# Attention scores with 64-row by 32-column TensorE tiles in place of zero-padded queries

## Chip, cores and metric

The kernel runs on one core of a Trainium2 chip. The metric is the device time of one execution in microseconds, as the median over runs. All times below are in microseconds (us) unless marked ns.

## What is computed

The program is three blocks in a row: a windowed attention, a mixture of experts and a dense block with a rational activation. The change touches the attention alone. Cut to it, the reference is

```python
B, H, Sl, D, Sg = 4, 8, 512, 64, 32
k_all, v_all = concat([k_g, k_l]), concat([v_g, v_l])
out_g = softmax(q_g @ k_all.T / 8) @ v_all             # 32 global tokens see everything
s_ll = q_l @ k_l.T / 8, kept where |i - j| <= 32        # local tokens see a window
s_lg = q_l @ k_g.T / 8                                  # and the 32 global tokens
out_l = softmax(concat([s_lg, s_ll])) @ concat([v_g, v_l])
attn = concat([out_g, out_l])                          # (4, 8, 544, 64)
x = attn as (2176, 512); x = experts(x); out = dense(x)
```

Everything is float32.

## The kernel before

**Tiling.** A batch has 512 local tokens, cut into 16 blocks of 32 (`W`). A block of queries needs 128 keys: three blocks of local keys and the 32 global ones. `KT[b]` holds the transposed keys: two heads of a pair stand on partitions 0 to 63 and 64 to 127, four pairs along the free axis, and the global keys are repeated between the local blocks so that 128 neighbouring columns are what a query block needs. `QB0` and `QB1` (`qb_t`, L305) hold the transposed queries, scaled by -1/8, of one half of a batch each. They are padded: for each pair and block there are two groups of 32 columns, the first with queries on partitions 0 to 63 and zeros below, the second the other way round. So one stationary operand of 128 rows by 64 columns gives the scores of both heads of a pair against their own keys.

**One unit** (`unit`, L565) is four query blocks of one batch, all eight heads; there are 4 per batch, 16 in all. It runs two halves `hg` of four heads. Each half takes one of four PSUM banks of the ring `sc`, adds the window mask by one bf16 matmul of 128x128 by 512 columns (L589), then runs 8 matmuls (L596) of 128x64 by 128 columns, each into 64 of the 128 partitions:

```python
nc.tensor.matmul(ps[64*j:64*j+64, n*128:(n+1)*128],
                 qb_t[u//2][:, 2*hg+j, u%2*4+n].rearrange("p a q -> p (a q)"),
                 KT[b][:, 2*hg+j, o:o+128], start=False, stop=True, ...)
```

The trace writes two records for each float32 matmul, so a half is 16 records of L596. `weights` (L604) then takes the row maximum on DVE (`mx`, L609), four exponentials on ACT (`A`, L285), frees the bank, transposes on PE (L627) and copies (`AT`). `values` multiplies with the value windows `VW` (L650: 32 float32 matmuls of 128x32 by 64 columns, four column groups), normalizes (L661, `xs`), stores to `xd`, and computes router logits (L679, L694, L703).

**Global queries.** `globals_of` (L714) does the same for the 32 global queries of a batch: per half two matmuls of 128x64 by 512 columns (L729) and two by 32 (L732), from `qgT`, which is zero-padded too. `prep_g` (L459) makes `kgT` and `qgT`: a copy that brings the heads into the order `ORD` (on DVE for k, on POOL for q, L464), four transposes (L471), copies out of PSUM on ACT.

**Order of work.** Nothing is left to a hardware scheduler. `Flow` is a planner that runs at build time: each piece of work is a Python generator that yields `(engine, us)` before it issues, and the planner keeps a clock for each engine and issues by rank and by earliest start. Its assumed costs therefore set the order on PE, ACT, DVE, POOL and SP, and each engine then works strictly in that order. A half of a unit's scores is planned as `("PE", 1.3)`. Transfers go through SP: keys, queries, values (`kr`, `qr`, `vr`), window copies from SBUF to SBUF (`VW<-vr`), stores (`xd`), and between them 24 pieces of the dense block's weights (`stg`, 512 KB each, three buffers), which ACT (L264) and DVE (L265 to L267) turn from 64-bit into 32-bit during the attention. The second planner run (router, experts, dense block) begins with a clock of its own and is issued after the attention's last PE and ACT instructions.

Of the kernel before, what the change touches and what calls it, by code (L numbers as in the profile page):

```python
# [66 lines left out]


class Flow:

# [18 lines left out]
    def _on(self, p, got=None):  # L89
        gen, rank, after, _ = p  # L90
        self.now = after
        while True:
# [5 lines left out]
            if isinstance(item, Ring):  # L98
                if item.waiters or not item.free():
                    item.waiters.append(p)  # L100
                    return
                got = self._take(item, after)
            elif isinstance(item, Slots):
# [85 lines left out]
def moe_kernel(ctx: ExitStack, tc: tile.TileContext, q_l, k_l, v_l, q_g, k_g, v_g, w_gate, w1, w2,  # L189
# [81 lines left out]
    with ExitStack() as actx:  # L271
# [186 lines left out]

        def prep_g(key, eng):  # L459
            yield g_in[key]  # L460
            yield eng, 0.6
            t, g = graw[key]
            src = raw.tile([128, H, D], F32, name=f"{key}g", tag="gr", bufs=1)
            (V if eng == "DVE" else nc.gpsimd).tensor_copy(src.rearrange("p (a c) d -> p a c d", a=2),  # L464
                                                           t.rearrange("p (c a) d -> p a c d", a=2))
            flow.fire(g)
            sc = yield sc_s
            p = bank("sc", 4)
            yield "PE", 0.436
            for pr in range(NP):  # L470
                nc.tensor.transpose(p[:, pr * 128:(pr + 1) * 128],  # L471
                                    src[:, 2 * pr:2 * pr + 2, :].rearrange("p h d -> p (h d)"), identf)
            p = p.rearrange("p (a s) -> p a s", a=NP)
            if key == "k":
                yield "ACT", 0.48
                act(kgT, p, AF.Copy)
            else:
                for h in range(2):
                    yield "ACT", 0.48
                    o = slice(64 * h, 64 * h + 64)  # L480
                    act(qgT[o, :, :, h], p[o].rearrange("p a (b q) -> p a b q", b=B), AF.Copy)
            flow.fire(g_t[key])
            flow.fire(sc)

        def pairs_T(src, s, put, done, rank):

            t = src.rearrange("p h (t d) -> p h t d", t=2)
            for par in range(2):
# [3 lines left out]
                for pr in range(NP):  # L492
                    for a in range(2):
                        nc.tensor.matmul(p[64 * a:64 * a + 64, pr * 128:(pr + 1) * 128], t[:, ORD[2 * pr + a], par],  # L494
                                         identf, start=True, stop=True)
# [11 lines left out]
        def both_T(src, s, put, done, rank):  # L507

            for a in range(2):
# [3 lines left out]
                for pr in range(NP):  # L513
                    nc.tensor.transpose(p[:, pr * 128:(pr + 1) * 128], src[:, ORD[2 * pr + a]], identf)
                if a:
# [37 lines left out]
        def prep_q(b, r, rank):  # L553
# [4 lines left out]
            t = qb_t[r]  # L558

            def put(a, par, rows, p):  # L560
                o = t[rows, :, :, a].rearrange("p a n (q t) -> p a n q t", t=2)
                copy(o[:, :, :, :, par], p.rearrange("p a (n q) -> p a n q", n=8), -scale)

# [3 lines left out]
        def unit(b, u, rank):  # L567
# [12 lines left out]
            flow.go(after(A_free, a), 0)  # L580
            flow.go(values(b, u, rank, at, sm, m, turned), rank)
            for hg in range(2):
                sc = yield sc_s
                ps = bank("sc", 4)
                yield "PE", 1.3
                m0 = 2 if u else 0
                ms = masks[:, m0:m0 + 4] if u in (0, NB // 4 - 1) else \
                    masks[:, None, m0:m0 + 2].to_broadcast([128, 2, 2, 128])
                nc.tensor.matmul(ps.rearrange("p (a n) -> p a n", n=128) if ms.ndim == 3 else  # L589
                                 ps.rearrange("p (a b n) -> p a b n", a=2, b=2), identh, ms,  # L590
                                 start=True, stop=False, skip_group_check=True)
                for n in range(4):
                    w0 = win(4 * u + n)
                    o = (w0 // 2 * 3 + w0 % 2) * W
                    for j in range(2):
                        nc.tensor.matmul(ps[64 * j:64 * j + 64, n * 128:(n + 1) * 128],  # L596
                                         qb_t[u // 2][:, 2 * hg + j, u % 2 * 4 + n].rearrange("p a q -> p (a q)"),
                                         KT[b][:, 2 * hg + j, o:o + 128], start=False, stop=True,
                                         skip_group_check=True)
                flow.fire(k_used[b, 0])  # L600
                flow.fire(q_used[b, u // 2])
                flow.go(weights(rank, hg, ps, sc, A[:, hg], mx[:, hg], sm, at, at_in, turned, A_free),
                        rank + 0.01 * hg)
# [105 lines left out]
        def globals_of(b, rank):  # L709
# [6 lines left out]
            for hg in range(2):  # L716
# [8 lines left out]
                yield "PE", 1.0  # L725
                lq = [qgT[:, 2 * hg + j, b].rearrange("p a q -> p (a q)") for j in range(2)]
                kt = sl(KT[b])[:, 2 * hg:2 * hg + 2]
                for j in range(2):
                    nc.tensor.matmul(ps[64 * j:64 * j + 64].rearrange("p (g s) -> p g s", s=2 * W), lq[j],  # L729
                                     kt[:, j, :, :2 * W], start=True, stop=True)  # L730
                for j in range(2):
                    nc.tensor.matmul(pg[64 * j:64 * j + 64, :SG], lq[j], kt[:, j, 0, 2 * W:], start=True, stop=True)  # L732
                flow.fire(k_used[b, 0])
# [117 lines left out]
        with tc.manual_schedule(engines={ET.PE, ET.Activation, ET.DVE, ET.SP, ET.Pool}):  # L851
            warm(W1)
            flow.clock["PE"] = 0.52 * W1
            flow.go(load_global(k_g, "k"), -9)
            flow.go(prep_g("k", "DVE"), -9)
            for b in range(B):
# [10 lines left out]
                if b == 0:  # L867
                    flow.go(load_global(q_g, "q"), 2 - LD[0])
                    flow.go(prep_g("q", "POOL"), 1)
                for u, n in ((0, i), (1, i + 1), (2, i + 3), (3, i + 4)):  # L870
# [902 lines left out]
```

## Time and profile before

| | |
|---|---|
| runs | 879.29 median of 3 (878.82 to 881.04) |
| the profiled execution | 881.8, of which 880.0 is its span |
| mean granted TensorE clock | 0.973 of full speed |
| busy share of the span | PE 94%, DVE 81%, ACT 57%, POOL 30% |
| attention | from the start to about 192 |

A group's row gives a line, an engine, the operation, the tile written and those read, sizes and count; behind the bar the busy time, the mean of one in ns, and idle time before the group with what ended it. Busy times of overlapping matmuls are merged. A timeline row gives start, length (first start to last end), engine, line, operation and count. A chain row gives start and length of a step on the chain of waits, which is followed back from the last instruction. A row of windows gives, for each stretch, busy time and count per engine, the granted clock (1.00 is 2.4 GHz, 0.50 is 1.2 GHz), the DMA engines' busy share and GB/s.

### The profile page before, as it was taken

How to read it: one execution, taken by the hardware profiler on the slowest of the kernel's cores; microseconds unless marked ns; L12 is line 12 of the kernel's file. 1: busy time of each engine (PE TensorE's matmuls, PEld its weight loads, DVE VectorE, ACT ScalarE, POOL GpSimd, SP SyncE). 2: the span in 40 equal slices, each digit the busy share in tenths (PEclk: the TensorE clock that was granted, in tenths of full speed). 3: DMA queues.
4: the chain of work that ended last, by engine and by line, in shares of the span. 5: the costliest groups of instructions: out<-in, count | busy, mean ns of one | idle time of the engine just before them, and what ended most of it. 6: DMA issues, size and time to landing. Idle time of an engine off the chain costs nothing.

```text
span 880.0 us, 20528 instructions
## 1 busy us (share of the span) xinstructions
PE 830.7 (94%) x7945; PEld 730.3 (83%) x7956; DVE 712.1 (81%) x1647; ACT 504.1 (57%) x1137; POOL 260.8 (30%) x227
## 2 busy tenths in 40 slices
PE   8887988879899999999999999999999999999997
PEld 5665766657689899999889999998999999998995
DVE  4557777758889989989998989999887767668985
ACT  4665676759544545545554554555455555556753
POOL 7510220000223334233442433334243343330001
PEclk9998997989999999999999999999999999999999
DMA  9989885623444222221331222133223122210000
GB/s 218 243 237 271 207 254 160 181 77 97 141 123 122 73 60 62 73 85 37 97 97 48 73 75 83 37 97 98 60 61 107 50 73 84 85 37 13 13 1 36
DMA packets 130538, 88.99 MB, mean 101 GB/s; under 512 B 28840, under 2 KB 119464, under 8 KB 130440
## 3 DMA queue, kind: packets, MB, share of 16 engines
q1 hardware_dynamic: 126632, 76.92, 31.6%
q0 software_dynamic: 3280, 10.75, 3.7%
q8 instruction: 62, 1.02, 0.5%
q14 instruction: 36, 0.29, 0.1%
q10 hardware_dynamic: 528, 0.02, 0.0%
HBM read 70.02 MB, written 8.92 MB: 90 GB/s over the span
## 4 chain that ended last, share of the span: by engine, by line
PE 65%; DVE 14%; issue 10%; DMA 6%; ACT 3%; SPq 2%; POOL 1%; DVEq 0%; POOLq 0%; ACTq 0%
PE sc L1244 6%; PE sc L1246 6%; PE sc L1245 5%; PE sc L1251 5%; PE sc L1249 5%; PE sc L1250 5%; PE tq L1244 5%; PE tq L1245 5%; PE tq L1246 5%; PE sc L596 3%; DMA stg<-in_moe_w_out_dram 2%; SPq L383 2%; PE sc L494 2%; PE tq L1355 2%; PE av L1019 2%
## 5 line engine op out<-in xcount | busy, mean ns | idle before, releaser
L1489 POOL TENSOR_TENSOR wlo<-rows,whi 128x512 fp32r<-128x512 f32 x120 | 168.0, 1402 | 333.3 <-ACT whi L1480 324.7
L1244 PE MATMUL tq<-yr,wh 128*128 128x256 f32 (+1 forms) x512 | 148.4, 290 | 1.5 <-DVE p L1632 1.5
L1245 PE MATMUL tq<-yr,wh 128*128 128x256 f32 (+1 forms) x512 | 147.4, 288 | 0.0
L1246 PE MATMUL tq<-yr,ws 128*128 128x256 f32 (+1 forms) x512 | 146.9, 287 | 0.0
L1249 PE MATMUL sc<-wh,t 128*128 128x512 f32 x248 | 99.9, 403 | 0.0
L1251 PE MATMUL sc<-wh,t 128*128 128x512 f32 x248 | 99.0, 399 | 0.8 <-DVE t L1660 0.7
L1244 PEld LDWEIGHTS tq<-yr,wh 128*128 128x128 f32 x512 | 96.5, 188 | 3.1 <-issue 2.2
L1250 PE MATMUL sc<-ws,t 128*128 128x512 f32 x248 | 97.9, 395 | 0.0
L1245 PEld LDWEIGHTS tq<-yr,wh 128*128 128x128 f32 x512 | 96.4, 188 | 0.8
L1246 PEld LDWEIGHTS tq<-yr,ws 128*128 128x128 f32 x512 | 96.6, 189 | 0.0
L1480 ACT ACTIVATE whi<-rows 128x512 fp32r<-128x512 f32 x120 | 75.1, 628 | 17.0 <-PE sc L1245 13.1
L1620 ACT ACTIVATE t<-tq,coef 128x512 f32<-128x512 f32 (+1 forms) x67 | 44.9, 670 | 52.5 <-PE tq L1246 40.9
L1524 ACT ACTIVATE hh<-sc 128x272 fp32r<-128x272 f32 x64 | 25.4, 397 | 86.4 <-PE sc L1246 86.1
L1244 PE MATMUL sc<-xhi,whi 128*128 128x272 f32 x240 | 72.9, 304 | 0.0
L1244 PE MATMUL sc<-hh,whi 128*128 128x272 f32 x240 | 70.6, 294 | 0.0
L1246 PE MATMUL sc<-xhi,wlo 128*128 128x272 f32 x240 | 69.6, 290 | 0.5 <-POOL wlo L1489 0.5
L1246 PE MATMUL sc<-hh,wlo 128*128 128x272 f32 x240 | 69.3, 289 | 0.0
L1245 PE MATMUL sc<-hl,whi 128*128 128x272 f32 x240 | 69.2, 288 | 0.0
L1245 PE MATMUL sc<-xlo,whi 128*128 128x272 f32 x240 | 69.1, 288 | 0.0
L1638 DVE SCALAR_TENSOR_TENSOR t<-t,b 128x512 f32<-128x512 f32 (+1 forms) x67 | 52.0, 776 | 20.3 <-ACT t L1622 20.2
L1641 ACT ACTIVATE t<-t,cq 128x512 f32<-128x512 f32 (+1 forms) x67 | 47.3, 706 | 23.4 <-DVE t L1638 23.2
L1251 PEld LDWEIGHTS sc<-wh,t 128*128 128x128 f32 x248 | 46.6, 188 | 15.9 <-DVE t L1660 5.2
(313 smaller groups left out, 2182.2 us busy)
## 6 DMA issues: line engine op xcount, KB each, us to landing
rows<-in_moe_w_dram SPq DMA_DIRECT2D x128, 256.0 KB, 2.8
stg<-in_moe_w_in_dram SPq DMA_DIRECT2D x16, 512.0 KB, 4.3
stg<-in_moe_w_out_dram SPq DMA_DIRECT2D x16, 512.0 KB, 7.8
VW<-vr SPq DMA_DIRECT2D x18, 256.0 KB, 3.2
kr<-in_k_l_dram SPq DMA_DIRECT2D x8, 512.0 KB, 5.9
qr<-in_q_l_dram SPq DMA_DIRECT2D x8, 512.0 KB
vr<-in_v_l_dram SPq DMA_DIRECT2D x16, 256.0 KB, 5.3
xd<-xs SPq DMA_DIRECT2D x64, 64.0 KB, 3.3
```

Of the source, the lines that this page charges most:

```text
L596: nc.tensor.matmul(ps[64 * j:64 * j + 64, n * 128:(n + 1) * 128], qb_t[u // 2][:, 2 * hg + j, u % 2 * 4 + n].rearrange("p a q -> p (a q)") ...
L1244: nc.tensor.matmul(ps, whi, xhi, start=first, stop=False)
L1245: nc.tensor.matmul(ps, whi, xlo, start=False, stop=False)
L1246: nc.tensor.matmul(ps, wlo, xhi, start=False, stop=last)
L1249: nc.tensor.matmul(ps, ghi, whi, start=first, stop=False)
L1250: nc.tensor.matmul(ps, ghi, wlo, start=False, stop=False)
L1251: nc.tensor.matmul(ps, glo, whi, start=False, stop=last)
L1480: nc.scalar.activation(hi, raw, AF.Copy)
L1489: (V if alt else nc.gpsimd).tensor_tensor(lo, raw, hi.bitcast(F32), op=OP.subtract)
L1620: nc.scalar.activation(q, ph, AF.Abs, scale=b0)
L1638: V.scalar_tensor_tensor(q, r, b1, q, op0=OP.mult, op1=OP.add)
L1641: nc.scalar.activation(r, q, AF.Ln, bias=cq)
```

## The change

Queries lose their zero padding. A stationary operand is now one head: 64 rows (its half of the partitions) by 32 columns. A half `hg` now means the four heads that lie on the same 64 partitions, one of each pair, rather than two pairs; so `ORD` disappears from the loads. Both halves of a unit are issued together: two banks are taken first (`Next` puts the second request at the head of the ring's queue), two masks follow, then 32 matmuls that alternate between the two halves of the partitions and between the two banks. `globals_of` uses the same tiles, one half after the other. The head-reordering copies of `prep_g`, the zero fills of `QB` and `qgT`, and one of the two ACT copies into `qgT` are gone. The planner's cost of a unit's scores goes from 2 x 1.3 to 2 x 0.3 + 1.0. Masks, exponentials, transposes and values keep their form.

```diff
-        qb_t = [ac.tile([128, NP, 8, 2, W], F32, name=f"QB{i}") for i in range(2)]
-        for t in qb_t:
-            nc.gpsimd.memset(t, 0.0)
+        qb_t = [ac.tile([128, NP, 8, W], F32, name=f"QB{i}") for i in range(2)]
...
-        qgT = ac.tile([128, NP, B, 2, W], F32, name="qgT")
+        qgT = ac.tile([128, NP, 128], F32, name="qgT")
...
-        nc.gpsimd.memset(qgT, 0.0)
...
-            yield eng, 0.6
-            src = raw.tile([128, H, D], F32, name=f"{key}g", tag="gr", bufs=1)
-            (V if eng == "DVE" else nc.gpsimd).tensor_copy(...)
...
-            if key == "k":
-                act(kgT, p, AF.Copy)
-            else:
-                for h in range(2):
-                    o = slice(64 * h, 64 * h + 64)
-                    act(qgT[o, :, :, h], p[o].rearrange("p a (b q) -> p a b q", b=B), AF.Copy)
+            act(kgT if key == "k" else qgT, p.rearrange("p (a s) -> p a s", a=NP), AF.Copy)
...
+            sc = [(yield sc_s), (yield Next(sc_s))]
+            ps = [bank("sc", 4) for _ in range(2)]
             for hg in range(2):
-                sc = yield sc_s
-                ps = bank("sc", 4)
-                yield "PE", 1.3
+                yield "PE", 0.3
                 nc.tensor.matmul(... identh, ms, start=True, stop=False, ...)
-                for n in range(4):
-                    for j in range(2):
-                        nc.tensor.matmul(ps[64 * j:64 * j + 64, n * 128:(n + 1) * 128],
-                                         qb_t[u // 2][:, 2 * hg + j, u % 2 * 4 + n].rearrange("p a q -> p (a q)"),
-                                         KT[b][:, 2 * hg + j, o:o + 128], ...)
+            yield "PE", 1.0
+            for n in range(4):
+                for j in range(NP):
+                    for hg in range(2):
+                        d = slice(64 * hg, 64 * hg + 64)
+                        nc.tensor.matmul(ps[hg][32 * j:32 * j + 32, n * 128:(n + 1) * 128],
+                                         qb_t[u // 2][d, j, u % 2 * 4 + n], KT[b][d, j, o:o + 128], ...)
...
-                lq = [qgT[:, 2 * hg + j, b].rearrange("p a q -> p (a q)") for j in range(2)]
-                for j in range(2):
-                    nc.tensor.matmul(ps[64 * j:64 * j + 64]..., lq[j], kt[:, j, :, :2 * W], ...)
+                lq = [qgT[64 * hg:64 * hg + 64, j, b * SG:(b + 1) * SG] for j in range(NP)]
+                for j in range(NP):
+                    nc.tensor.matmul(ps[32 * j:32 * j + 32]..., lq[j], kt[:, j, :, :2 * W], ...)
```

The planner's new costs change the order on every engine in the attention. The first place is PE, batch 0, where units 2 and 3 follow the global queries (`Ag` is the global weights, `ATg` their transpose). Before:

```order
L765 MATMUL tx<-identf,Ag 32x128
L589 LDWEIGHTS identh
L589 MATMUL sc<-masks,identh 128x512
L596 MATMUL sc<-KT,QB_97 64x128 x8
L589 LDWEIGHTS identh
L589 MATMUL sc<-masks,identh 128x512
L596 MATMUL sc<-KT,QB_97 64x128 x8
L761 MATMUL tq<-identf,Ag 128x128 x4
L793 MATMUL av<-vr,ATg 32x64 x16
```

and with the change:

```order
L769 MATMUL tx<-identf,Ag 32x128
L588 LDWEIGHTS identh
L588 MATMUL sc<-masks,identh 128x512
L588 LDWEIGHTS identh
L588 MATMUL sc<-masks,identh 128x512
L598 MATMUL sc<-KT,QB_97 32x128 x32
L698 MATMUL tx<-XT,wg 32x128 x4
L765 MATMUL tq<-identf,Ag 128x128 x4
L797 MATMUL av<-vr,ATg 32x64 x16
```

The two banks are now both written before either half's scores are complete, and the 16 matmuls of two halves have become 32 in one run.

The second place is SP, the queue that issues the transfers, from the first weight pieces (`stg`) of batch 0 on. Before:

```order
L261 DMA stg_465<-in_moe_w_in_dram 128x1024
L383 DMA xd<-xs 32x4x128 x4
L383 DMA kr<-in_k_l_dram 128x8x128
L383 DMA VW<-vr 64x2x512
L383 DMA qr<-in_q_l_dram 128x8x128
L383 DMA VW<-vr 32x2x512
L383 DMA xd<-xs 32x4x128
```

and with the change:

```order
L273 DMA stg_476<-in_moe_w_in_dram 128x1024
L392 DMA xd<-xs 32x4x128 x4
L392 DMA kr<-in_k_l_dram 128x8x128
L273 DMA stg_541<-in_moe_w_in_dram 128x1024
L392 DMA VW<-vr 64x2x512
L392 DMA VW<-vr 32x2x512 x2
L392 DMA qr<-in_q_l_dram 128x8x128
```

The third weight piece has moved ahead of the window copies of batch 1. The transfers themselves, their number and their sizes stay the same, and behind the attention every engine keeps its order.

## Rows read from the trace of the kernel before

**Rows 1.** Windows: attention in two parts, and the rest.

```profile
0.00:125.00 125.00, 107.69 (x1688) 80.51 (x1696) 79.12 (x188) 77.99 (x263) 38.33 (x39) 0.92 0.93 236
125.00:192.00 67.00, 52.93 (x1013) 40.14 (x1015) 46.60 (x196) 44.38 (x161) 7.83 (x10) 0.91 0.54 150
192.00:880.00 688.00, 670.13 (x5249) 609.66 (x5248) 586.37 (x1264) 381.77 (x714) 214.68 (x178) 0.99 0.24 72
```

**Rows 2.** Groups of PE's matmuls, from 0 to 191.

```profile
L596 PE MATMUL sc<-KT,QB 128*64 128x128 f32 x512 | 38.3, 296 | 2.2 <-ACT KT L285 0.4 <-issue 0.4
...
L650 PE MATMUL av<-VW,AT 128*32 128x64 f32 x1024 | 20.7, 227 | 3.6 <-ACT AT L285 3.6
...
L729 PE MATMUL sc<-KT,qgT 128*64 128x512 f32 x32 | 9.5, 676 | 0.0
```

**Rows 3.** PE's timeline: one unit's halves, one unit's values, global scores.

```profile
41.75 0.38 PE L589 MATMUL sc<-masks,identh 128*128 128x512 bf16 x1
42.06 1.09 PE L596 MATMUL sc<-KT,QB 128*64 128x128 f32 x16
43.09 0.39 PE L589 MATMUL sc<-masks,identh 128*128 128x512 bf16 x1
43.41 1.09 PE L596 MATMUL sc<-KT,QB 128*64 128x128 f32 x16
...
50.65 1.10 PE L650 MATMUL av<-VW,AT 128*32 128x64 f32 x64
51.68 0.66 PE L627 MATMUL tq<-identf,A 128*128 128x128 f32 x4
```

**Rows 4.** Chain of waits, from 0 to 190: transfers, and scores.

```profile
18.56 6.95 DMA kr<-in_k_l_dram
...
42.13 1.02 PE sc L596 x16
...
51.15 6.30 DMA stg<-in_moe_w_in_dram
...
76.70 7.60 DMA stg<-in_moe_w_out_dram
...
89.86 1.83 PE sc L596 x16
...
119.45 5.68 DMA stg<-in_moe_w_out_dram
...
164.51 4.98 DMA stg<-in_moe_w_out_dram
...
174.00 1.09 PE sc L596 x16
```

**Rows 5.** Two ten-microsecond windows in which the clock is low.

```profile
80.00:90.00 10.00, 7.29 (x97) 4.49 (x99) 5.72 (x12) 4.60 (x14) 2.54 (x2) 0.56 0.99 315
130.00:140.00 10.00, 6.08 (x67) 4.65 (x70) 7.73 (x16) 5.27 (x19) 1.00 (x1) 0.62 0.68 171
```

**Rows 6.** Timelines of DVE, POOL and ACT: the copies and fills that go.

```profile
4.41 0.48 DVE L464 COPY kg<-kgr 128x512 f32<-128x512 f32 x1
...
11.30 3.41 POOL L455 COPY VW<-vg 32x2048 f32<-32x2048 f32 x2 [5.03 <-DMA vg<-in_v_g_dram]
...
23.43 0.61 POOL L464 COPY qg<-qgr 128x512 f32<-128x512 f32 x1
...
30.35 1.19 ACT L285 ACTIVATE qgT<-sc 64x512 f32<-64x512 f32 x2 [0.22 <-PE sc L471]
```

**Rows 7.** ACT's timeline: first and fourth exponential of one half.

```profile
23.57 0.37 ACT L285 ACTIVATE A<-sc,mx 128x128 f32<-128x128 f32 x1
...
24.61 0.37 ACT L285 ACTIVATE A<-sc,mx 128x128 f32<-128x128 f32 x1
```

**Rows 8.** Waits from 0 to 190 (waiter, line, cause: total, times, longest).

```profile
DVE mx L609 <- PE sc L596: 21.6, 16, 3.7
...
ACT stg L264 <- DMA stg<-in_moe_w_out_dram: 9.0, 5, 3.2
```

More of the change, by code (lines that the diff above doesn't have):

```diff
@@ L66, in free, with __init__ @@
         return k < 0 or self.taken[k].at
+class Next:
+    def __init__(self, ring):
+        self.ring = ring
 class Flow:
@@ L102, in _on @@
                 got = self._take(item, after)
+            elif isinstance(item, Next):
+                if not item.ring.free():
+                    item.ring.waiters.insert(0, p)
+                    return
+                got = self._take(item.ring, after)
             elif isinstance(item, Slots):
@@ L456, in globals_, with prep_g @@
                 flow.fire(done)
-        def prep_g(key, eng):
+        def prep_g(key):
             yield g_in[key]
-            yield eng, 0.6
-            t, g = graw[key]
-            src = raw.tile([128, H, D], F32, name=f"{key}g", tag="gr", bufs=1)
-            (V if eng == "DVE" else nc.gpsimd).tensor_copy(src.rearrange("p (a c) d -> p a c d", a=2),
-                                                           t.rearrange("p (c a) d -> p a c d", a=2))
-            flow.fire(g)
             sc = yield sc_s
@@ L558, in prep_q @@
             t = qb_t[r]
+            o = t.rearrange("p a n (q t) -> p a n q t", t=2)
             def put(a, par, rows, p):
-                o = t[rows, :, :, a].rearrange("p a n (q t) -> p a n q t", t=2)
-                copy(o[:, :, :, :, par], p.rearrange("p a (n q) -> p a n q", n=8), -scale)
+                copy(o[rows, :, :, :, par], p.rearrange("p a (n q) -> p a n q", n=8), -scale)
             yield from both_T(*qraw[b, r], put, q_t[b, r], rank)
@@ L603, in unit @@
+            flow.fire(k_used[b, 0])
+            flow.fire(k_used[b, 0])
+            flow.fire(q_used[b, u // 2])
+            flow.fire(q_used[b, u // 2])
+            for hg in range(2):
+                flow.go(weights(rank, hg, ps[hg], sc[hg], A[:, hg], mx[:, hg], sm, at, at_in, turned, A_free),
                         rank + 0.01 * hg)
@@ L725, in globals_of @@
                 yield "PE", 1.0
-                lq = [qgT[:, 2 * hg + j, b].rearrange("p a q -> p (a q)") for j in range(2)]
-                kt = sl(KT[b])[:, 2 * hg:2 * hg + 2]
-                for j in range(2):
-                    nc.tensor.matmul(ps[64 * j:64 * j + 64].rearrange("p (g s) -> p g s", s=2 * W), lq[j],
+                lq = [qgT[64 * hg:64 * hg + 64, j, b * SG:(b + 1) * SG] for j in range(NP)]
+                kt = sl(KT[b])[64 * hg:64 * hg + 64]
+                for j in range(NP):
+                    nc.tensor.matmul(ps[32 * j:32 * j + 32].rearrange("p (g s) -> p g s", s=2 * W), lq[j],
                                      kt[:, j, :, :2 * W], start=True, stop=True)
-                for j in range(2):
-                    nc.tensor.matmul(pg[64 * j:64 * j + 64, :SG], lq[j], kt[:, j, 0, 2 * W:], start=True, stop=True)
+                for j in range(NP):
+                    nc.tensor.matmul(pg[32 * j:32 * j + 32, :SG], lq[j], kt[:, j, 0, 2 * W:], start=True, stop=True)
                 flow.fire(k_used[b, 0])
@@ L854, in moe_kernel @@
             flow.go(load_global(k_g, "k"), -9)
-            flow.go(prep_g("k", "DVE"), -9)
+            flow.go(prep_g("k"), -9)
             for b in range(B):
@@ L868, in moe_kernel @@
                     flow.go(load_global(q_g, "q"), 2 - LD[0])
-                    flow.go(prep_g("q", "POOL"), 1)
+                    flow.go(prep_g("q"), 1)
                 for u, n in ((0, i), (1, i + 1), (2, i + 3), (3, i + 4)):
```

33 lines of the change are left out of this document (15 added, 18 removed).

## The prediction

> **What bounds the kernel now.** I read the windows first, to see which stage the change can touch and with what the stage is full. The attention fills 0 to 192 us and is followed by 688 us in which PE is busy for 670 [rows 1]. The order of every engine behind the attention stays as it was, the second planner run starts from a clock of its own, and the transfers there take 0.24 of the DMA engines, so an earlier end of the attention should carry through to the end about one to one. Within the attention no engine is full: up to 125 us PE is busy 107.7 of 125 and the DMA engines 0.93 of the time; from 125 to 192 us PE is busy 52.9 of 67 and DMA 0.54 [rows 1].
>
> Next the groups, for PE's share. The scores (L596) are its largest group in the attention, 38.3 us over 32 halves [rows 2]. The timeline gives a clean one: 16 records between 42.06 and the next mask at 43.09, so 1.03 us, or 64 ns a record [rows 3]. The record itself lasts 296 ns [rows 2], so neighbours overlap: two column groups of 64 work side by side.
>
> Last the chain of waits, to see how much of that is on the path. Up to 190 us it runs through 19 of the 32 score halves, from the one at 42.13 to the one at 174.00; three of them ran at a low clock, like the one at 89.86, which took 1.83 us. Between them it waits for transfers: the keys at 18.56 (6.95 us) and weight pieces at 51.15, 76.70 and 119.45 (6.30, 7.60, 5.68) [rows 4]. So PE and DMA take turns on the path, and time saved on PE ahead of such a transfer is kept only if the transfer comes earlier too.
>
> **The change, part by part.**
>
> *The score matmuls.* A unit had 2 x 16 records of L596 in 2 x 1.03 = 2.06 us. It will have 32 matmuls, so 64 records, each 32 stationary columns wide and 128 moving columns long. The trace has the same count and width in a unit's values: 64 records of L650 between 50.65 and 51.68, 1.03 us, 16 ns each, with 64 moving columns and four column groups side by side [rows 3]. The new records stream twice as many columns, but there are eight tiles instead of four, if the two halves of the partitions work side by side as well. Then the same 1.03 us comes out, and the scores fall from 38.3 to L650's 20.7 us, 17.6 us less PE work [rows 2]. If the halves of the partitions take turns, each record costs twice L650's, 64 x 32 ns = 2.06 us, the same as now and no gain. No row before the change shows matmuls on two halves of the partitions at once; these are the two ends. I take 1.03 us, because the count, the width and the number of operand elements read per unit of time are those of L650, whose four groups do overlap in full.
>
> The Trainium skill ("TensorEngine Tiling (Array Packing)", Key Properties) says that different tiles can execute weight loads and matmuls in parallel, which would give the lower end; no row here shows it for tiles above one another.
>
> *Global scores.* Half the rows, half the columns, twice the matmuls of 512 columns. Per half 4 records on two column groups become 8 on four, and a half still follows its twin; 9.5 us in all now [rows 2], and I cost the difference at nothing. L729 is covered by no other work, but the streamed columns per group stay the same.
>
> *Masks.* Still 32 of them, at 0.31 to 0.32 us from start to start [rows 3]. Two now stand together, and PE changes its tile shape once a unit less. I cost that at nothing.
>
> *Copies and fills that go.* The DVE copy for k takes 0.48 us at 4.41, POOL's for q 0.61 us at 23.43, one of two ACT copies at 30.35 (1.19 us for the two) [rows 6]. After the fills POOL sat idle for 5.03 us waiting for values from DRAM, so the fills were hidden [rows 6]. PE still waits for the keys that land at 25.5 (18.56 + 6.95) [rows 4], so the copies at 4.41 and 23.43 are hidden as well; the ACT copy is beside a PE that is busy. Together nothing on the path. If the key transfer were earlier, the next cover is PE's own work.
>
> *Moved transfers.* The third weight piece goes onto SP's queue ahead of the window copies of batch 1. That may shorten the wait at 51.15 [rows 4], but the copies behind it, and the stores queued behind those, come later by a piece's share. I cost it at nothing with either sign.
>
> *The sum.* On the chain, 16 halves at full clock save 1.03 - 0.52 = 0.51 us each and three slow ones half of 1.83, 0.9 us each: 16 x 0.51 + 3 x 0.9 = 10.9 us. That is the most the path can give. Against it stand the transfers. Up to 125 us the DMA engines are busy 0.93 of the time, 116 us of work that remains; at the 0.99 share of the fullest stretch, 80 to 90 us [rows 5], it would still need 117 us, so at most 8 us can go there, and sustained 0.99 is unlikely. Also, when PE runs ahead and then waits longer for a transfer, it comes back slow: behind such waits the granted clock is 0.56 at 80 to 90 us and 0.62 at 130 to 140 us [rows 5], near the 1.2 GHz level, where PE's work costs twice. I take half of 10.9, 5.4 us. From the profiled execution's 881.8 us that gives 876.4. That execution lies 2.5 us above the median of the three runs (879.29), so in terms of the median I predict **873.9 us**.
>
> **The rivals.**
>
> *Everything to its end.* If the transfers follow PE, the whole 10.9 us is kept: 879.29 - 10.9 = 868.4. For it: after 125 us DMA is at 0.54 [rows 1]. Against it: 14 of the 19 halves lie before 125 us.
>
> *The transfers set the end.* Only the five halves on the chain after 125 us count, one of them slow: 4 x 0.51 + 0.9 = 2.9 us; half of that is lost in the waits behind them, as the piece at 119.45 shows before them [rows 4]. About 1.5 us, 877.8: no difference that the runs can tell. For it: 0.93 before 125 us. Against it: SP issues a weight piece only when DVE and ACT have freed its buffer, and they wait for PE.
>
> *The two partition halves take turns,* so the change doesn't do what it says. Scores cost 2.06 us a unit as now, the chain is as now, and the planner, which believes in 1.0 us, places what follows too early. 879 within a microsecond. For it: nothing in the trace shows the overlap. Against it: the overlap of column groups is full [rows 3].
>
> *PE waits for a second bank: slower.* A unit now needs two of the four `sc` banks before it can run any matmul of its scores, and a bank is freed by the fourth exponential of a half, 24.61 - 23.57 + 0.37 = 1.41 us after the first one starts [rows 7]. The two banks of the unit before are freed about that far apart, and everything behind the second mask in PE's order waits. If that happens in half of the 16 units, it costs 8 x 1.41 = 11.3 us on PE. Set against the 5.4 us it would leave +6, 885. It decides if PE comes to the second mask less than 1.41 us after the first bank was freed. For it: the sixteen waits of L609 for scores, 21.6 us [rows 8], show that DVE and ACT follow close behind PE, and a faster PE closes up. Against it: L596's group has 2.2 us of idle time before it in the whole attention [rows 2], none of it for a bank. A milder form, a third of the units, gives 881.
>
> The Trainium skill ("TensorEngine Tiling (Array Packing)", Gotcha 1: PSUM Pressure) speaks for this rival: row tiles must write to different banks and so raise the pressure on PSUM. The trace of before agrees only so far as that the banks are four and no wait for one is seen.
>
> **How the numbers follow.** A measurement of this kernel can tell 0.3%, 2.6 us, from no change: faster is under 876.7, slower over 881.9. Forecast 0.42, all to its end 0.12, transfers set the end 0.18, halves take turns 0.12, second bank 0.16. Faster takes nine tenths of the forecast and all of the second, 0.50, and some of the third: 0.53. Slower takes two thirds of the bank's case, 0.11, and some of the changed order in the others: 0.18. Same has 0.29. The range reaches from the full gain, 868.4, less about 1 us for a shorter wait at 51.15, to the bank's case below its 885: 867 to 883.
>
> **What would show it.** The new score group has 1024 records; right is a start-to-start of some 16 ns in it and about 1.0 us a unit, and a group near 21 us; wrong is 2.06 us a unit and about 38. The attention should end near 187 in place of 192, the DMA share up to 120 us should rise above 0.93, and the waits for weight pieces should stay about as long. Idle time before the mask matmuls released by ACT's exponentials would show the bank rival. [...] The prediction is wrong if PE's scores halve and the attention's end stays at 192, or if the stretch behind the attention changes its length.

## The result and the profile after

The changed kernel takes **885.28 us** (median of 5 runs, 885.06 to 885.85); the kernel before, run beside it, 880.64 us (5 runs, 878.82 to 881.04). The ratio is 1.006, 95% interval 1.0045 to 1.0074: slower by over 0.3%, where 873.9 was predicted and 867 to 883 was the range. The profiled execution has a span of 883.8 us at a mean granted clock of 0.965; before it was 880.0 at 0.973.

The windows show the stage, the columns as in [rows 1]. The third row of this fence is the part behind the attention, the last one a stretch that lies inside the attention of both kernels. After:

```profile
0.00:125.00 125.00, 102.34 (x2041) 72.02 (x2042) 77.90 (x182) 75.00 (x259) 34.59 (x35) 0.89 0.91 231
125.00:197.00 72.00, 53.26 (x1243) 37.22 (x1241) 49.30 (x199) 44.63 (x165) 8.10 (x10) 0.86 0.55 150
197.00:884.00 687.00, 669.30 (x5252) 609.80 (x5252) 587.02 (x1265) 381.66 (x714) 214.66 (x178) 0.99 0.24 72
20.00:190.00 170.00, 137.33 (x3044) 98.15 (x3044) 115.48 (x330) 109.46 (x405) 33.23 (x30) 0.87 0.77 206
```

The same stretch in the kernel before:

```profile
20.00:190.00 170.00, 143.22 (x2550) 109.66 (x2561) 116.59 (x341) 112.59 (x400) 32.08 (x31) 0.91 0.77 207
```

What follows the attention is nearly unchanged: 687 us with 669 us of PE, against 688 and 670 [rows 1]. The loss is all in the attention. The first warm-up matmul behind it starts at 191.35 us before and at 197.25 after, 5.9 us later; the spans differ by 3.8, as what follows that matmul took 2.1 us less in this execution. In the common stretch PE is busy 5.9 us less, at a granted clock of 0.87 in place of 0.91.

The groups of PE's matmuls, 0 to 200 us, after:

```profile
L631 PE MATMUL tq<-identf,A 128*128 128x128 f32 x128 | 25.5, 319 | 2.2 <-ACT A L297 2.0
L598 PE MATMUL sc<-KT,QB 64*32 64x128 f32 x1024 | 24.3, 318 | 4.0 <-issue 4.0
L492 PE MATMUL sc<-identf,kr 128*64 128x128 f32 x256 | 18.1, 290 | 0.1
L683 PE MATMUL tx<-identf,xs 128*128 128x128 f32 x64 | 11.6, 310 | 14.4 <-DVE xs L665 14.3
L733 PE MATMUL sc<-KT,qgT 64*32 64x512 f32 x64 | 9.4, 658 | 0.0
L698 PE MATMUL tx<-XT,wg 128*32 128x128 f32 x128 | 8.0, 327 | 5.0 <-ACT XT L297 5.0
```

The four of them that the change leaves alone, before:

```profile
L627 PE MATMUL tq<-identf,A 128*128 128x128 f32 x128 | 21.8, 299 | 0.0
L494 PE MATMUL sc<-identf,kr 128*64 128x128 f32 x256 | 17.2, 285 | 4.0 <-DMA kr<-in_k_l_dram 4.0
L679 PE MATMUL tx<-identf,xs 128*128 128x128 f32 x64 | 10.7, 292 | 5.9 <-DVE xs L661 5.9
L694 PE MATMUL tx<-XT,wg 128*32 128x128 f32 x128 | 7.0, 293 | 6.3 <-ACT XT L285 6.2
```

So the change did what it says: the scores fall from 38.3 us [rows 2] to 24.3, by 14.0 us. But the same other matmuls take longer: 3.7 + 0.9 + 0.9 + 1.0 = 6.5 us more in these four groups, with the clock lower. And PE waits 14.3 us in place of 5.9 for `xs`, the attention output that DVE scales.

PE also stands idle for 4.0 us inside the score matmuls of two units, when both banks are already taken. The profile shows nothing that it waited for, and no run looked for the cause. Before, idle time of this kind was 0.4 us [rows 2].

```profile
90.14 0.62 PE L598 MATMUL sc<-KT,QB 64*32 64x128 f32 x19 [2.63 <-issue]
153.57 0.63 PE L598 MATMUL sc<-KT,QB 64*32 64x128 f32 x22 [1.34 <-issue]
```

The timeline shows how a unit now runs (start us, duration us, engine and line). After:

```profile
48.97 0.59 PE L588 MATMUL sc<-masks,identh 128*128 128x512 bf16 x2
49.49 1.16 PE L598 MATMUL sc<-KT,QB 64*32 64x128 f32 x64
51.09 1.28 DVE L613 TENSOR_REDUCE mx<-sc 128x4 f32<-128x512 f32 x2
52.91 0.36 ACT L297 ACTIVATE A<-sc,mx 128x128 f32<-128x128 f32 x1
```

And the row maxima and the first exponential of the unit of [rows 3], before:

```profile
43.51 0.68 DVE L609 TENSOR_REDUCE mx<-sc 128x4 f32<-128x512 f32 x1
44.29 0.37 ACT L285 ACTIVATE A<-sc,mx 128x128 f32<-128x128 f32 x1 [0.49 <-DVE mx L609]
44.71 0.68 DVE L609 TENSOR_REDUCE mx<-sc 128x4 f32<-128x512 f32 x1
```

64 records of the new tile take 1.16 us, 17 ns from start to start. With 128 rows in place of 64 (e4 below, where no two halves can overlap) a clean unit's 64 records take 2.0 us, so the two halves of the partitions do overlap. The Trainium skill says that different tiles can run matmuls in parallel ("TensorEngine Tiling (Array Packing)", Key Properties); the trace agrees. But before, the first half's maxima began 1.45 us after its scores (42.06 to 43.51), while PE was at the second half, and its first exponential 2.23 us after them. Now both halves finish together, the maxima begin at 1.60 us and the first exponential at 3.42 us.

Single units vary, so here are the means over all sixteen, read off the timelines: from a unit's first score record to its first row maximum, to its first and last exponential, and from one unit's first score to the next one's (us).

| kernel | first maximum | first exponential | last exponential | unit to unit |
|---|---|---|---|---|
| before | 1.70 | 3.25 | 9.16 | 10.58 |
| after | 2.44 | 4.20 | 8.62 | 10.85 |

PE's work per unit fell by nearly 0.9 us (14.0 / 16), and units still follow each other 0.27 us later. Over 15 distances that is 4.1 us; the first unit's scores start 1.0 us earlier (14.34 against 15.33), so the last unit's start 3.2 us later.

The end of the attention shows the other 2.7 of the 5.9 us. ACT's last unit (its first and last exponential, and the last `XT`) and PE's last scores, before:

```profile
176.98 1.09 PE L596 MATMUL sc<-KT,QB 128*64 128x128 f32 x16
177.42 0.36 ACT L285 ACTIVATE A<-sc,mx 128x128 f32<-128x128 f32 x1
183.22 0.41 ACT L285 ACTIVATE A<-sc,mx 128x128 f32<-128x128 f32 x1
189.37 0.60 ACT L285 ACTIVATE XT<-tx 128x512 f32<-128x512 f32 x1 [2.49 <-PE tx L679]
191.35 0.59 PE L235 MATMUL sc<-onesb 128*128 128x512 bf16 x1
```

After:

```profile
177.15 1.16 PE L598 MATMUL sc<-KT,QB 64*32 64x128 f32 x64
180.25 0.36 ACT L297 ACTIVATE A<-sc,mx 128x128 f32<-128x128 f32 x1
188.18 0.37 ACT L297 ACTIVATE A<-sc,mx 128x128 f32<-128x128 f32 x1
195.04 0.60 ACT L297 ACTIVATE XT<-tx 128x512 f32<-128x512 f32 x1 [3.53 <-PE tx L683]
197.25 0.59 PE L247 MATMUL sc<-onesb 128*128 128x512 bf16 x1
```

The last scores end at 178 us in both kernels: the 14 us of PE are gone by then. But before, the last unit's first half had been scored from 174.00 [rows 4] and its exponentials were already running; after, all eight come behind 178, the first 2.8 and the last 5.0 us later, and the rest of the chain follows at the same distance.

The waits, 0 to 200 us (columns as in [rows 8]), after:

```profile
ACT XT L297 <- PE tx L683: 21.9, 11, 5.1
DVE mx L613 <- PE sc L598: 18.5, 8, 4.2
PE tx L683 <- DVE xs L665: 14.3, 7, 3.6
ACT A L297 <- DVE mx L613: 12.3, 6, 6.1
```

Before, the two of ACT that [rows 8] doesn't have:

```profile
ACT XT L285 <- PE tx L679: 11.9, 5, 3.6
ACT A L285 <- DVE mx L609: 6.1, 8, 1.9
```

ACT's waits for the maxima and for the transposes of `xs` double, or nearly so. No wait of the mask matmuls (L588) for a bank appears.

### The profile page after: what moved, and what is told of

Same layout as the page of the kernel before. It is cut to its first block, busy times and chain, and to the rows that moved or that the text cites. A ratio compares the mean times of both kernels' runs of the same rounds, so it can differ in the third digit from the quotient of the medians.

```text
span 883.8 us, 21674 instructions
## 1 busy us (share of the span) xinstructions
PE 824.9 (93%) x8532; PEld 719.0 (81%) x8532; DVE 714.2 (81%) x1646; ACT 501.3 (57%) x1136; POOL 257.3 (29%) x223
## 4 chain that ended last, share of the span: by engine, by line
PE 62%; DVE 17%; issue 10%; DMA 4%; ACT 4%; SPq 2%; POOL 1%; DVEq 0%; POOLq 0%; ACTq 0%
PE sc L1248 6%; PE sc L1250 6%; PE sc L1249 6%; PE tq L1248 5%; PE sc L1255 5%; PE tq L1249 5%; PE tq L1250 5%; PE sc L1253 5%; PE sc L1254 5%; DMA stg<-in_moe_w_in_dram 2%; SPq L392 2%; PE sc L598 2%; PE av L1023 2%; DVE wide_a L1019 1%; PE tq L631 1%
```

## The experiments

Ratios are to the kernel before, run beside each on the same chip, with 95% intervals. "Attention's end" is the start of the first warm-up matmul in the profiled execution (191.35 before, 197.25 after).

### First round: POOL's copies, the planner's cost, the padding

A view of DVE gave the first theory. In the kernel after, an instruction on `ws` (L278) that took 0.69 us at 59.81 took 2.31 at 62.96, and one on `rs` 1.43 (0.17 at 85.62), ahead of `xs`, while POOL copied `VW<-vg`:

```profile
62.84 3.76 POOL L464 COPY VW<-vg 32x2048 f32<-32x2048 f32 x2 [22.10 <-PE av L654]
62.96 2.31 DVE L278 SCALAR_TENSOR_TENSOR ws<-stg,ws 128x512 int32<-128x512 int32 x1
65.20 1.43 DVE L662 TENSOR_SCALAR rs<-sm 128x8 f32<-128x8 f32 x1
67.34 0.68 DVE L665 TENSOR_TENSOR xs<-av,rs 128x512 f32<-128x512 f32 x1
```

**Cut POOL's copies** into one per window, in the kernel after (e1) and in that before (e2):

```
-                nc.gpsimd.tensor_copy(dst, src)
+                for c in range(k):
+                    nc.gpsimd.tensor_copy(dst[:, c:c + 1], src[:, c:c + 1])
```

> The changed kernel, with POOL's copies of the global values into the windows cut into one copy per window (about 0.45 us each in place of two of 1.7 to 2.0 us); nothing else, and the planned order on PE is the same. Theory POOL: while one of these copies runs, DVE's instructions that work on SBUF alone stand still until it ends, and in the changed kernel they stand ahead of xs at six places out of six (two before), so that L683 waits 14.3 us for xs where it waited 5.9. Then the waits of L683 for xs fall to 8 us or less and the time from 885.3 to about 879 (877 to 882). Theory ORDER (the planner's new order itself puts weight pieces ahead of what PE waits for, whatever POOL does): 884 to 886, waits of L683 within 2 us of 14.3. Theory CLOCK (the saved PE time only turned into idle time with a low clock behind it): 884 to 886, too.

> The kernel before with the same cut of POOL's copies and nothing else. Theory POOL: only two of its six copies delay an xs that PE waits for, so it gains less than the changed kernel does from the same cut: 1 to 3 us, 878 to 879.5, and the waits of L679 for xs fall from 5.9 to about 3 us. Theories ORDER and CLOCK: 880 to 881, no change.

Measured: e1 882.85 us, 1.0013 (0.9976 to 1.0049), `xs` waits down from 14.3 to 11.1 us, attention's end 195.75. e2 877.78 us, 0.998 (0.9955 to 1.0005), waits from 5.9 to 3.2. The copies cost both kernels about as much, some 2 to 3 us. They are real, and not what parts the two.

**The planner told 2.0 us** for the new score matmuls in place of 1.0, in the kernel after (e3):

```
-            yield "PE", 1.0
+            yield "PE", 2.0
```

> The changed kernel with the planner told 2.0 us in place of 1.0 us for a unit's score matmuls, so 2.6 us with the masks as before the change; the instructions are the same, their order on all engines is another. Theory ORDER: back to 880 or below, because the order comes near to what the old costs gave. Theory POOL: the time goes with the number of POOL copies that fall on DVE's work ahead of xs, 878 to 885, and the waits of L683 for xs tell which. Theory CLOCK: 884 to 887, PE still idles as much.

Measured: 893.45 us, 1.0137 (1.0105 to 1.0169), attention's end 203.29. That the loss comes from the planner now believing in a shorter time is not borne out; a longer one makes it worse, and the same instructions in another order cost 8 us more.

**Zero-padded tiles of 128 rows and 32 columns** in the kernel after, its order kept (e4): no overlap between partition halves, so PE pays for the scores nearly as before. The zero fills of `QB` come back with it.

```
...
-                                         qb_t[u // 2][d, j, u % 2 * 4 + n], KT[b][d, j, o:o + 128],
+                                         qb_t[u // 2][:, j, u % 2 * 4 + n, hg], KT[b][:, j, o:o + 128],
...
```

> The changed kernel with zero-padded queries again, 128 rows by 32 columns: the same 32 matmuls a unit in the same planned order, but no two of them on different halves of the partitions at once. A unit's scores should take about 2.0 us in place of 1.09. If PE's time is what the attention hangs on (as the prediction had it), the time rises by 5 to 11 us, to 890 to 896. If the xs chain on DVE sets the pace (theory POOL), PE's extra 1 us a unit goes into its waits for xs in good part: 886 to 889. Theory CLOCK: PE idles less, the clock stays up, 884 to 886.

Measured: 888.67 us, 1.008 (1.0046 to 1.0113); score group 35.3 us against 24.3, attention's end 197.57 against 197.25, though in an execution 2.3 us under its median; by the two ratios it is some 2 us slower than the change, with intervals that overlap. Eleven microseconds more PE work cost some 2 us. Little of the new tile's gain is on the path.

### Second round: weight pieces and small costs

**Light weight pieces**, before (e5) and after (e6): ACT's step and the last two of DVE's three are left out of each piece.

```
-            tail[:] = [a()]
             for f, t in zip(d, (0.335, 0.6, 0.6)):
                 yield "DVE", t
-                f()
+                if f is d[0]:
+                    f()
```

> The kernel before, planned in the same order, with the ACT instruction and the last two of the three DVE instructions of each weight piece left out of the attention (24 pieces; the dense block's weights are then not converted). The transfers of the pieces stay. It is the yardstick for the next run. If DVE's pieces cost the attention little before the change, it ends 2 to 4 us earlier than the 191 us of before; the total follows, about 877.

> The changed kernel with the same instructions left out, planned in the changed order. Theory PIECES (in the changed order weight pieces stand on DVE ahead of xs, and PE waits for them): the attention ends 6 us or more earlier than its 197, and not later than in the yardstick run; the total falls to 878 or less and to no more than that run's. Theory ORDER (the changed order is worse in more than the pieces: halves issued together, transfers, transposes): it stays 3 us or more behind the yardstick run.

Measured: e5 872.94 us, 0.9893 (0.9854 to 0.9933), attention's end 184.16; e6 876.92 us, 0.995 (0.9925 to 0.9976), end 188.05. Less work on ACT and DVE shortens the attention, which no cut in PE's score work did, and the difference between the two orders stays: 4 us. So the steps left out are not what parts the two.

**Small changes of cost**: 0.8 for 1.3 a half in the kernel before (e7), 1.2 for 1.0 a unit in that after (e8).

```
-                yield "PE", 1.3
+                yield "PE", 0.8
```

> The kernel before, its padded tiles and half-by-half issue, with the planner told 0.8 us a half in place of 1.3 (so 1.6 a unit, as the change tells it). PE's work is what it was; only the order changes. Theory ORDER: any order but the one that the constants were chosen for costs several us, so 884 to 890 with no new tile at all. Theory JOINT (the loss comes from taking both halves and two banks at once): 880 to 882, since halves are still issued one by one.

> The changed kernel with the planner told 1.2 us in place of 1.0 for a unit's score matmuls: nearer to the 1.09 us that the trace shows, a small step in the order. Theory ORDER: a spread of some us either way, 880 to 890. Theory JOINT: within 1.5 us of the changed kernel, 884 to 887, as both halves still go together.

Measured: e7 882.64 us, 1.0016 (0.9982 to 1.005); e8 888.25 us, 1.0084 (1.0048 to 1.0119). A small change of the plan alone moves the time by some 2 to 3 us, and the larger one of e3 moved it by 8. The change's own loss of 4.6 us is of that size, so a difference like it between two orders carries no mechanism by itself. Those below of 11 and 15 us lie above it, but they too contain a new order.

### Third round: what the saved PE time is worth, and the joint start

**Half the scores left out** in the kernel before, its own order kept (e9): two of four blocks' score matmuls.

```
-                for n in range(4):
+                for n in (0, 2):
```

> The kernel before, in its own order on every engine, with every second query block's score matmuls left out (blocks 1 and 3 of a unit get the mask alone), so 8 records of L596 a half in place of 16 and some 0.5 us less PE time a half, 16 us in all: as much as the change takes off PE, without its joint issue and its order. If PE's score time is on the path as the prediction's sum had it (10.9 us on the chain, half of it kept), the time falls by 3 to 8 us, to 872 to 877, and the attention ends at 184 to 188 in place of 191. If transfers, DVE and ACT set the pace whatever PE does, it stays within 1.5 us: 879 to 882. It tells whether the prediction's gain was there to be had at all.

Measured: 880.82 us (10 runs) beside 881.04 (29): 0.9998 (0.998 to 1.0016). In the profiled execution, 1.7 us above that median, the attention's end is 193.72. PE's groups in it, 0 to 197 us:

```profile
L596 PE MATMUL sc<-KT,QB 128*64 128x128 f32 x256 | 23.1, 306 | 0.4 <-ACT KT L285 0.4
L627 PE MATMUL tq<-identf,A 128*128 128x128 f32 x128 | 23.2, 314 | 0.0
L650 PE MATMUL av<-VW,AT 128*32 128x64 f32 x1024 | 22.1, 235 | 4.6 <-ACT AT L285 3.5 <-issue 1.1
L494 PE MATMUL sc<-identf,kr 128*64 128x128 f32 x256 | 19.0, 304 | 5.4 <-DMA kr<-in_k_l_dram 5.4
```

Its window from 20 to 190 us:

```profile
20.00:190.00 170.00, 137.87 (x2313) 99.87 (x2309) 117.42 (x340) 112.12 (x405) 32.91 (x31) 0.87 0.78 206
```

And PE's wait for `xs`:

```profile
PE tx L679 <- DVE xs L661: 10.8, 6, 3.2
```

This is the run that decides the prediction's sum. PE lost 15.2 us of score work at a fixed order of every engine, and the time did not move (the interval leaves room for 1.8 us of gain at most). One sees where it went: the waits for `xs` rise from 5.9 to 10.8 us, and the clock from 20 to 190 us falls from 0.91 to 0.87. The same other matmuls take longer: 1.4 us for `tq`, 1.4 for `av`, 1.8 for the keys' transposes. Both are the signs that the kernel after shows.

**Joint start with the old tile** (e10): the 128x64 tile, but a unit takes both banks, then both masks, all 16 score matmuls, then launches both softmax chains, as the change does.

```
...
+            sc = [(yield sc_s), (yield Next(sc_s))]
+            ps = [bank("sc", 4) for _ in range(2)]
             for hg in range(2):
-                sc = yield sc_s
-                ps = bank("sc", 4)
-                yield "PE", 1.3
...
+                yield "PE", 0.3
...
+            yield "PE", 2.0
+            for hg in range(2):
...
+            for hg in range(2):
+                flow.go(weights(rank, hg, ps[hg], sc[hg], A[:, hg], mx[:, hg], sm, at, at_in, turned, A_free),
```

> The kernel before with its padded 128x64 tiles, its head order and its planned 2.6 us a unit, but with the change's joint issue: both banks are taken first, both masks written, then the 16 score matmuls of the two halves, and only then do both halves' softmax chains begin. Theory JOINT: it is this that costs the time, by making every unit wait for two free banks and by starting two halves' exponentials at once: 888 or more, about as the changed kernel with the same planned 2.6 us (893.5), and the last scores to the attention's end take 18 us or more in place of 13. Theory ORDER (any new set of planner costs loses some us, joint or not): 880 to 886, since the costs are the old ones.

Measured: 896.29 us, 1.0172 (1.0138 to 1.0207), attention's end 212.84, `xs` waits 17.0 us. The joint issue with the old tile costs 15 us; with the new tile at the same planned 2.0 us (e3) it costs 13. At this plan the loss goes with the joint issue, not with the tile. Why a planned 2.0 us costs 8 us more than a planned 1.0 on the same tile (e3 against the change) was not followed up.

**WR from 5.0 to 6.0** in the kernel after (e11): the weight pieces rank later.

```
-WR = (5.0, 0.67)
+WR = (6.0, 0.67)
```

> The changed kernel with the weight pieces ranked one unit later in the planner (6.0 in place of 5.0 for the first). Nothing else. Theory JOINT: the loss stays, 883 to 889. Theory ORDER: another order, anything from 878 to 890; under 880 would say that the change only needed its constants set anew.

Measured: 884.12 us, 1.0038 (1.0014 to 1.0062). Some 1 to 2 us less than the change; the constant alone was not the trouble.

**e2 again, with more runs** (e12):

> The kernel before with POOL's copies of the global values cut into one copy per window, as in the second run, timed with more rounds since it is a candidate that may beat both kernels: 877 to 879.5 against 880 to 881, a ratio of 0.997 to 0.999. If the first reading was the spread of the runs, the ratio is 1.000.

Measured: 878.2 us (12 runs) beside 881.04 (29): 0.9971 (0.9948 to 0.9993). By its median this is the fastest kernel with the whole computation, and it has the old tile. POOL's timeline in it has seven pieces where two copies were:

```profile
61.45 4.04 POOL L456 COPY VW<-vg 32x512 f32<-32x512 f32 x7 [21.09 <-PE av L651]
```

The wait for `xs` that was 5.9 us:

```profile
PE tx L680 <- DVE xs L662: 1.2, 2, 1.0
```

### Fourth round: banks or softmax, and the rest

**Banks first** (e13): both banks taken before the first mask, all else half by half as before.

```
...
+            sc = [(yield sc_s), (yield Next(sc_s))]
+            ps = [bank("sc", 4) for _ in range(2)]
             for hg in range(2):
-                sc = yield sc_s
-                ps = bank("sc", 4)
                 yield "PE", 1.3
...
```

**Late softmax** (e14): banks one by one as before, but the first half's softmax is launched only behind the second half's matmuls.

```
+            held = []
             for hg in range(2):
...
+                held.append((ps, sc))
+            for hg, (ps, sc) in enumerate(held):
                 flow.go(weights(rank, hg, ps, sc, A[:, hg], mx[:, hg], sm, at, at_in, turned, A_free),
```

> The kernel before, tiles, costs and half-by-half issue as they were; only both banks of a unit are taken before its first mask. Theory BANKS (waiting for two free banks of four is what the joint issue costs): 890 or more, close to the 896 of the joint issue. Theory START (the late start of the first half's softmax costs it): 880 to 884.

> The kernel before with banks taken one by one and the halves issued as they were, but the planner lets the first half's softmax begin only after the second half's matmuls are issued. Theory START: 890 or more, close to 896. Theory BANKS: 880 to 884.

Measured: e13 879.23 us, 0.9981 (0.9959 to 1.0004); e14 892.37 us, 1.0136 (1.0089 to 1.0183). With the old tile the banks cost nothing; the late launch, with the order that the planner makes of it, costs 11 us. The means over sixteen units, formed as above:

| kernel | first maximum, us | first exponential, us | ratio to before |
|---|---|---|---|
| e13, banks first | 1.66 | 3.04 | 0.9981 |
| before | 1.70 | 3.25 | 1 |
| after | 2.44 | 4.20 | 1.006 |
| e4, padded 32 columns | 2.53 | 4.21 | 1.008 |
| e15, WR 6 and cut copies | 2.32 | 4.27 | 0.9976 |
| e3, planned at 2.0 | 2.54 | 3.88 | 1.0137 |
| e10, joint, old tile | 3.14 | 4.58 | 1.0172 |
| e14, late softmax | 4.18 | 6.23 | 1.0136 |

All the slow kernels of this table start the first half's softmax late, but the loss does not follow the delay: e3 and e14 lose the same with very different delays, and e15 (below), with the change's tile and joint issue, starts as late as the change and loses nothing. How the lateness comes about is not the same in each. In the change the matmuls themselves are interleaved, so no half can be early. In e14 the data are there early, as one unit shows:

```profile
49.52 1.98 PE L597 MATMUL sc<-KT,QB 128*64 128x128 f32 x16
51.55 0.69 DVE L612 TENSOR_REDUCE mx<-sc 128x4 f32<-128x512 f32 x1 [4.76 <-PE sc L597]
52.33 0.37 ACT L285 ACTIVATE A<-sc,mx 128x128 f32<-128x128 f32 x1 [0.20 <-DVE mx L612]
...
53.05 0.39 PE L590 MATMUL sc<-masks,identh 128*128 128x512 bf16 x1
```

The first half's maxima here run before the second half's mask. So much of e14's mean delay is probably the order that the planner writes for DVE and ACT once it learns of the softmax later. How much of the change's 5 us is the data and how much that order was not separated: no run kept the change's order with the halves' matmuls apart.

**After, with WR 6 and cut copies** (e15), the best of the small edits together:

> The changed kernel with the weight pieces ranked one unit later and POOL's copies cut into one copy per window. If the two gains seen apart (884.1 and 882.9 against 885.3) add up: 880 to 882, not better than the kernel before with its copies cut (878.2). If the cut takes away what ate the PE gain: under 877.

Measured: 879.19 us, 0.9976 (0.9949 to 1.0002). Tuned round about, the new tile comes level with the kernel before, and its interval overlaps e12's, so the two can't be told apart. Its first exponential comes 4.27 us after the first score, against 3.13 in e12: with these constants and cut copies the late start has no price that these runs can see. So the late start alone does not make the loss; it needs the change's order, POOL's copies, or both.

**Half the scores left out of e2** (e16), to see whether PE's time counts once POOL's copies are out of the way:

> The kernel before with POOL's copies cut up and every second block's score matmuls left out, in its own order: the ninth run's 15 us less PE time on top of the cut. Theory POOL (its copies in front of xs on DVE eat the PE time saved): clearly under the cut alone, 870 to 875 against 878.2. Theory SLACK (DVE, ACT and the transfers keep pace with PE anyway, whatever POOL does): 876 to 880, as with the cut alone.

Measured: 878.3 us, 0.9969 (0.9938 to 1.0), where e2 and e12 had 0.998 and 0.9971. The profiled execution, 4.6 us above the median, ends the attention at 192.08. PE's time still counts for nothing.

## Why the prediction was wrong

**Right: the stage and its carry.** What lies behind the attention kept its length, and the 5.9 us that the attention's end moved went through to the end nearly whole (4.6 us in the medians, 3.8 in the profiled spans).

**Right, a little off in size: the score matmuls.** 1.03 us a unit was predicted; 1.09 us came from start to start in a clean unit (49.49 to the next record at 50.58), 17 ns a record. The group is 24.3 us where L650's 20.7 was taken, at a lower mean clock; the same matmuls are busy for 21.7 us in the executions of e1 and e3. "The two partition halves take turns" is out. The global scores were costed at nothing and measured 9.4 us against 9.5.

**Wrong: "The sum".** It took 19 score halves from the chain of waits, called 10.9 us the most that the path can give, and kept half. e9 took 15.2 us of score work out at a fixed order, more than the change does, and the time moved by 0.02%. The term was worth nothing there, and nothing with POOL's copies cut (e16); in the change's order 11 us were worth some 2 (e4). The chain that is followed back names what ended last at each step. It does not say that the next-late thing is far behind, and here it is close: without the score time, PE waits for `xs`, and the clock falls. The step named the second way of losing ("it comes back slow") and gave it no figure of its own: the granted clock from 20 to 190 us fell by 0.04, which over the 137 us that PE is busy there is some 5.5 us of full-speed time (an estimate), against 14.0 us saved. e5 shows the contrast: taking work off ACT and DVE did shorten the attention. Two of the step's readings are off as well. The stretch of 80 to 90 us is not the fullest by share: from 30 to 40 the DMA engines stand at 1.00. And PE's own waits at the two slow windows were for ACT (2.73 us up to 79.91, 2.71 up to 85.53) and for `xs` from DVE (3.38 us up to 133.17), with the transfers of [rows 4] further back on the chain; from 170 to 180 and 180 to 190 PE is busy no more than in those windows, 7.2 and 6.3 us, and the clock is 1.00.

**Missing: the joint start and its order.** The part-by-part list costed masks, copies and transfers, but not that the interleaved matmuls and the one place of launch hold back the first half's maxima until the second half is scored, nor the new order on DVE and ACT. With the sum at nothing the forecast would have been no change; the 4.6 us lost fall to this missing term, or in part to the 4.0 us in which PE stood idle inside score matmuls. With the old tile e10 and e14 price such a start, together with the order planned for it, at 15 and 11 us, more than the prediction's whole gain. How the 4.6 us divide stays open: e3 loses 8 us more by its order alone, and e15 keeps the joint start and loses nothing.

**The rival "PE waits for a second bank"** gave 885 and so the right number, by luck, for a reason that falls: the masks wait for no bank in the trace, and taking two banks first costs nothing with the old tile (e13). The Trainium skill's warning about PSUM ("TensorEngine Tiling (Array Packing)", Gotcha 1) has no price that these runs show; none prices it with row tiles. The place was right, a unit issued whole where a half was issued before; but ACT and DVE are late by it, and PE behind them.

**"The transfers set the end"** came nearer than the forecast in that PE's time was worth next to nothing, but its reason is not borne out: e5 moves the same transfers, and its attention ends 7.2 us earlier. DMA's share up to 125 us, which the forecast wanted above 0.93, is 0.91.

## What to carry to other kernels

Before a saving on a followed-back chain is counted, find out what is late next: leave the work out at a fixed order and time it. If that changes nothing, a faster way of doing that work will not help at that order. When two halves are fused to feed one engine better, look at the engines that lived on the first half: they now start when the second is done. Here that start went with a loss of 13 or 15 us where a unit was planned at 2.0 us (e3, e10), of 5 in the change and of none in e15, so it has to be timed together with the order.

## What was not expected of the hardware

A POOL copy holds up certain DVE instructions until it ends. In the rows of the first round two copies run, the first from 62.84 to 64.73, the second from 64.79 to 66.60. The instruction on `ws` ends at 65.27, 0.54 us after the first copy, and the one on `rs` at 66.63, as the second copy ends. Two instructions that read PSUM were not held up: `xs` at 130.94 and the global maxima `m` at 131.54 took 0.68 and 0.67 us beside a pair of copies that ran from 128.59 to 132.34. The Trainium skill calls the port pair that the two engines share an exclusive lock held for the full instruction ("SBUF — State Buffer", Who interferes with whom); the trace agrees, and cutting the copies into pieces of some 0.6 us (4.04 us for seven) gave 0.3% (e12) with no work removed.

Less work on PE brought a lower clock: 0.87 for 0.91 between 20 and 190 us, both in the changed kernel and in e9. Over all runs the median clock of the execution is 0.9645 in e9 beside 0.976, and e4, which gives the changed kernel 11 us of PE work back, has 0.9745 in place of 0.966. In the 29 runs of the kernel before beside e9, too, the time goes with the mean granted clock: 875.45 us at 0.979 and 876.77 at 0.984, 884.8 at 0.972 and 885.66 at 0.970. Whether the clock is the cause there or only follows PE's idle time is not shown.
